# Loading the first eight chunks in 768-byte pieces, with conversion on GpSimd and two row copies per chunk

## The chip, the cores and the metric

The kernel runs on one core of a Trainium2 chip. The metric is the device time of one execution in microseconds. Three runs of the kernel before took 1412.79, 1413.59 and 1414.21 us; their median is 1413.59.

The engines are TensorE (PE in the rows; its weight loads are PEld), VectorE (DVE), ScalarE (ACT), GpSimd (POOL) and SyncE (SP). SyncE computes nothing here: it issues the DMAs. Every engine works through its own instructions in program order.

## The reference

Three stages follow one another. Inputs q, k, v and alpha have shape 4 x 8 x 768 x 48 (batch, head, time, dimension).

```
for t in range(S):                                  # gated linear attention
    state = alpha[t][:, None] * state + outer(k[t], v[t])
    y[t]  = q[t] @ state
x = y as 3072 x 384                                 # tokens x (head, dimension)
x = (sigmoid(x @ w_gate) * (x @ w_val)) @ w_out     # 384 -> 1536 -> 384
p = domain_probs / domain_probs.sum(-1)
out = sum over 4 experts of p[:, e] * (relu(x @ w1[e]) @ w2[e])   # 384 -> 1024 -> 384
```

Everything is float32. The gate weights are scaled up by 6.956, so the sigmoid is steep and the products before it must be accurate.

## The kernel before

**Split products.** A float32 product is made of three faster ones: every operand is kept as a high part and a low part (high x high, high x low, low x high). So each operand has to be split: ScalarE writes the high part, VectorE or GpSimd the low part as a difference.

**Chunks.** The recurrence runs over 24 chunks of 128 time steps (6 per batch). A chunk is handled in three stages. Stage 1 brings alpha, k and q into the layout head-and-dimension by time (heads in pairs, 64 rows for each head, of which 48 are used), forms running products of alpha forwards and backwards by two scans (`s1_a`, line 249, and `s1_b`, line 243) and multiplies them into q and k. Stage 2 (`s2_pe`, `s2_ev`) makes the masked scores q k. Stage 3 (`s3_pe`) adds the carried state's part and the scores' part into y; `s3_state` and `st_decay` carry the state on. For chunks 0 to 7 stage 1 turns the data on TensorE: `s1_t` transposes four 128 x 128 tiles per tensor with line 227. The later chunks arrive in pieces of four time steps and are turned on VectorE in 32 x 32 blocks.

**From y to tokens.** `s3_y` copies y out of the accumulator (line 311). It has four pairs of heads, but the next stage wants 3 x 128 rows, so the 48 rows per half of the fourth pair are moved into the unused 16 rows of the three others, by DMA from one place of on-chip memory to another (line 315, six of them per chunk). `s4` then splits the result: high part on ScalarE (line 341), low part on line 343, by VectorE for chunks 0 to 7 and by GpSimd later.

**Weights of the middle stage.** The 36 units (for each of 12 steps a gate, a value and an output slice) arrive as raw 32-bit words in four landing buffers (`load_w`; the gate and value units in four DMAs each, lines 177 and 180) and are decoded on the way. `dec_pre` makes two ScalarE passes (line 197 on the low 16-bit halves, line 199 turning the high halves from bfloat16 to float16 in place), `dec_bits` one on VectorE (line 203) that joins them, `dec_hi` (line 216, ScalarE) and `dec_lo` (line 219, VectorE) split. One call of `dec` does one pass for each of four successive units: hi of unit n-2, lo of n-3, pre of n, bits of n-1, and then `flush_w` issues the load of the unit that takes the buffer just freed.

**Order.** The order is written out by hand. Chunks 0 to 4 come first, in a loop over g whose iteration runs stage 1 of chunk g+1, stages 2 and 3 of chunk g, the split of chunk g-2 and one `dec`. The loop is called the prologue here. Six blocks of 512 tokens follow, each of 12 steps: gate products (18 with the value products, through `gv`), the sigmoid (line 393), the multiplication (line 397), its split (lines 398 and 402) and the output products of the step before (`l2`). In block 0 the remaining decodes are spread over the steps, and chunks 5 to 7 with one stage to a step; chunks 8 to 23 follow in blocks 1 to 4. Then the experts run, on TensorE almost without a gap. Block 0's step 0 needs the split of chunk 3; its step 1 can only overwrite the gate accumulator when the sigmoid of step 0 has read it.

All DMAs stand in SyncE's queue, so a load that comes behind a row copy in the program waits until that copy's data is there.

## Time and profile before

| what | us |
|---|---|
| median of 3 runs | 1413.59 |
| the profiled execution | 1413.35 |
| its span | 1411.6 |
| TensorE busy in the span | 1369.7 (97%) |
| VectorE busy | 708.8 (50%) |
| ScalarE busy | 406.3 (29%) |
| GpSimd busy | 104.3 (7%) |

The busy shares are means over stretches that differ. In the 40 slices of the span TensorE is at nine tenths or more in all but a few of the first five, and the DMA engines are busy most in the same slices. So the rows below look mostly at the first 170 us. The prologue lasts until about 53 us. Block 0's step 0 begins at 53.21 and its step 1 at 66.94; block 0 ends near 168.7 (the run of 54 products that starts at 160.38 and takes 12.48 us holds 36 of block 0 and 18 of block 1). In the rows a plain float32 product counts twice, once for each of its two passes, a transpose once.

### The profile page before, as it was taken

The page shows a single profiled execution, that of the slowest core. Times are in us where ns is not written, and L with a number is a line of the kernel's source. Part 1 is how long each engine was busy: PE and PEld are TensorE (multiplying, and loading weights), DVE is VectorE, ACT ScalarE, POOL GpSimd, SP SyncE. Part 2 cuts the span into 40 slices and gives each one's busy share as a digit, 9 for nine tenths or more (in the row PEclk, how much of TensorE's full clock was granted, in tenths as well). Part 3 has the DMA queues.
Part 4 walks back from the last instruction along what each step waited for, and adds up shares of the span by engine and source line. Part 5 has one row for each costly group of instructions (what it writes and reads, how often), then busy time and mean ns, then how long its engine had stood idle before and what let it go on. Part 6 is the DMA issues. An engine that isn't in the chain of part 4 may idle for free.

```text
span 1411.6 us, 19056 instructions
## 1 busy us (share of the span) xinstructions
PE 1369.7 (97%) x7600; PEld 1191.9 (84%) x7600; DVE 708.8 (50%) x1134; ACT 406.3 (29%) x794; POOL 104.3 (7%) x115
## 2 busy tenths in 40 slices
PE   8588999999999999999999999999999999999998
PEld 7467788788888888789999999999999999999997
DVE  6456777656565542244444444444444444444444
ACT  4587633333333333331111111111111111111111
POOL 0000000000000001430110011011011101101000
PEclk9899999999999999999999999999999999999999
DMA  9785422323232202130000000000000000000003
GB/s 128 128 172 134 115 71 74 85 61 76 72 79 71 75 4 97 53 97 0 23 23 1 23 23 23 0 23 23 0 23 23 12 12 23 0 0 1 1 29 109
DMA packets 116368, 70.19 MB, mean 50 GB/s; under 512 B 61488, under 2 KB 110896, under 8 KB 116272
## 3 DMA queue, kind: packets, MB, share of 16 engines
q1 hardware_dynamic: 116272, 68.90, 20.3%
q8 instruction: 62, 1.02, 0.3%
q14 instruction: 34, 0.28, 0.1%
HBM read 59.03 MB, written 8.65 MB: 48 GB/s over the span
## 4 chain that ended last, share of the span: by engine, by line
PE 84%; DMA 4%; issue 3%; ACT 3%; SPq 3%; DVE 2%; POOL 1%; ACTq 0%; POOLq 0%; DVEq 0%
PE bank L133 81%; PE bank L294 2%; SPq L315 1%; DMA LD<-in_moe_w_gate_dram 1%; ACT LD L199 1%; DMA LD<-LD 1%; DMA FA<-in_q_dram 1%; PE bank L274 1%; POOL RR L422 0%; DMA LD<-in_moe_w_val_dram 0%; DVE FA L243 0%; ACT RR L216 0%; ACT LD L267 0%; DMA LD<-in_moe_w_dram 0%; ACT LD L197 0%
## 5 line engine op out<-in xcount | busy, mean ns | idle before, releaser
L133 PE MATMUL bank<-RR 128*128 128x512 f32 (+1 forms) x5976 | 1262.2, 372 | 26.4 <-ACT LD L393 12.3
L133 PEld LDWEIGHTS bank<-RR 128*128 128x128 f32 x5976 | 1092.4, 189 | 184.4 <-ACT LD L393 14.0
L438 ACT ACTIVATE RR<-bank 128x512 fp32r<-128x512 f32 x192 | 114.7, 598 | 647.1 <-PE bank L133 647.1
L439 DVE SCALAR_TENSOR_TENSOR RR<-bank,RR 128x512 fp32r<-128x512 f32 x192 | 132.6, 691 | 330.7 <-ACT RR L438 330.7
L455 DVE SCALAR_TENSOR_TENSOR FA<-bank,pn,FA 128x384 f32<-128x384 f32 x360 | 221.6, 616 | 99.9 <-PE bank L133 99.9
L397 DVE TENSOR_TENSOR LD<-bank,LD 128x512 f32<-128x512 f32 x72 | 49.7, 691 | 171.9 <-PE bank L133 151.2
L422 POOL TENSOR_TENSOR RR<-LD,RR 128x384 fp32r<-128x384 f32 x64 | 63.5, 1020 | 641.1 <-PE bank L133 609.5
L393 ACT ACTIVATE LD<-bank 128x512 f32<-128x512 f32 x72 | 43.4, 602 | 140.0 <-PE bank L133 140.0
L398 ACT ACTIVATE RR<-LD 128x512 fp32r<-128x512 f32 x72 | 45.4, 631 | 115.2 <-DVE LD L397 115.1
L402 DVE TENSOR_TENSOR RR<-LD,RR 128x512 fp32r<-128x512 f32 x72 | 49.6, 689 | 11.7 <-ACT RR L398 11.2
L163 DVE STREAM_TRANSPOSE FA<-FA 128x512 f32<-128x512 f32 x48 | 51.9, 1081 | 0.0
L343 POOL TENSOR_TENSOR RR<-LD,RR 128x384 fp32r<-128x384 f32 x16 | 18.9, 1182 | 379.2 <-ACT RR L341 258.5
L133 PE MATMUL bank<-FA 48*128 48x128 f32 (+1 forms) x704 | 41.2, 259 | 0.1
L133 PEld LDWEIGHTS bank<-FA 48*128 48x128 f32 (+1 forms) x704 | 35.5, 167 | 6.3 <-issue 4.6
L199 ACT ACTIVATE LD<-LD 128x384 f16<-128x384 bf16 x36 | 38.1, 1059 | 0.0
L285 DVE TENSOR_TENSOR FA<-bank,mask 128x512 int32<-128x512 int32 x48 | 30.9, 684 | 11.6 <-PE bank L133 11.6
L243 DVE TENSOR_TENSOR_SCAN FA<-FA,LD 128x516 f32<-128x516 f32 x24 | 29.6, 1233 | 12.4 <-ACT FA L236 7.7
L249 DVE TENSOR_TENSOR_SCAN FA<-FA,LD 128x516 f32<-128x516 f32 x24 | 31.9, 1330 | 0.0
L203 DVE SCALAR_TENSOR_TENSOR LD<-LD 128x384 int32<-128x384 int32 x36 | 20.0, 555 | 16.1 <-ACT LD L199 13.7
L421 ACT ACTIVATE RR<-LD 128x384 fp32r<-128x384 f32 x64 | 28.0, 513 | 0.0
L334 ACT ACTIVATE St<-St,dk 128x128 f32<-128x128 f32 x80 | 25.4, 388 | 4.5 <-DVE St L329 2.7
L267 ACT ACTIVATE bank<-FA 128x512 f32<-128x512 f32 x38 | 23.3, 613 | 11.3 <-DVE FA L249 10.7
(63 smaller groups left out, 411.1 us busy)
## 6 DMA issues: line engine op xcount, KB each, us to landing
LD<-in_moe_w_dram SPq DMA_DIRECT2D x32, 384.0 KB, 3.3
FA<-in_alpha_dram SPq DMA_DIRECT2D x64, 96.0 KB, 2.3
FA<-in_k_dram SPq DMA_DIRECT2D x64, 96.0 KB, 2.4
FA<-in_q_dram SPq DMA_DIRECT2D x64, 96.0 KB, 2.3
FA<-in_v_dram SPq DMA_DIRECT2D x24, 192.0 KB, 3.0
LD<-in_moe_w_out_dram SPq DMA_DIRECT2D x12, 384.0 KB, 3.8
out_dram<-FA SPq DMA_DIRECT2D x24, 192.0 KB, 1.9
x2d<-LD SPq DMA_DIRECT2D x15, 256.0 KB, 2.2
```

Source lines behind the costliest of these rows:

```text
L133: nc.tensor.matmul(o, lhsT=l, rhs=r, start=start, stop=stop)
L163: nc.vector.transpose(out.rearrange("p a (t c) -> p a c t", c=TQ), t[:, BL:].rearrange("p (a d) -> p a d", d=D)[:, :, 0:BL])
L199: nc.scalar.activation(h[:, :, 1].bitcast(F16), h[:, :, 0].bitcast(BF16), AF.Copy)
L249: nc.vector.tensor_tensor_scan(flat(Iv), Ar[:, 0:NP * PW], flat(Cs), 1.0, ALU.mult, ALU.max)
L393: nc.scalar.activation(sg[f % 2], bank[0], AF.Sigmoid)
L397: nc.vector.tensor_tensor(s, bank[1], s, ALU.mult)
L398: nc.scalar.activation(gs[f % 2][0], s, AF.Copy)
L402: nc.vector.tensor_tensor(gl, sg[f % 2], gh.bitcast(F32), ALU.subtract)
L422: nc.gpsimd.tensor_tensor(lo, l[:, cs], h.bitcast(F32), ALU.subtract)
L438: nc.scalar.activation(h, bk, AF.Relu)
L439: nc.vector.scalar_tensor_tensor(l, bk, 0.0, h.bitcast(F32), ALU.max, ALU.subtract)
L455: nc.vector.scalar_tensor_tensor(acc[:, tt, :], bk, pn[:, tt, e:e + 1], acc[:, tt, :], ALU.mult, ALU.add)
```

## The change

Five things change. Chunks 0 to 7 are loaded like the later ones, in pieces of four time steps (768 bytes): a partition holds four successive time steps of one pair of heads, in two DMAs per tensor instead of one. `s1_t` turns them by products with the identity, eight per tensor, each of which takes one time step of four (c) and one head of a pair (j) and writes its 128 columns into the accumulator at their places (steps of 4 and 128 columns). For chunks 0 and 1 the second halves are issued from ScalarE's queue.

The pass from bfloat16 to float16 moves from ScalarE to GpSimd. The row copies become one per half, since the fourth pair's rows are dealt out in threes (`(p c)` in place of `(c p)`), and the weight rows are loaded in the matching order. The first decode runs in iteration 1 of the prologue instead of 2, with units 0 and 1 loaded in iteration 0 and 2 and 3 in iteration 1, and one decode fewer follows the loop. The load of the probabilities moves into block 1 and their division into block 2.

```diff
--- before.py
+++ after.py
@@ -79,9 +79,9 @@
 
 
     HW = 64
-    qn = [carve(FA, 512 * i, H, HW) for i in (0, 1)]
-    kn = [carve(FA, 512 * i, H, HW) for i in (2, 3)]
-    an = [carve(FA, 512 * i, H, HW) for i in (4, 5)]
+    qn = [carve(FA, 512 * i, 512) for i in (0, 1)]
+    kn = [carve(FA, 512 * i, 512) for i in (2, 3)]
+    an = [carve(FA, 512 * i, 512) for i in (4, 5)]
     vn = [carve(FA, 512 * i, H, HW) for i in (6, 7)]
     qt = [carve(FA, 512 * i, NP, P) for i in (8, 9)]
     kt = [carve(FA, 512 * i, NP, P) for i in (10, 11)]
...
@@ -138,25 +139,27 @@
         mm(o, ll, rh, False, stop)
 
 
-    def load(g, part, eng=nc.sync):
+    def load(g, part, engs=(nc.sync, nc.sync)):
         if g >= NCH:
             return
         b, c = divmod(g, CPB)
         i = g % 2
         ts = slice(c * P, (c + 1) * P)
         if part:
-            eng.dma_start(out=vn[i][:, :, 0:D], in_=v[b, :, ts, :].rearrange("h p d -> p h d"))
+            nc.sync.dma_start(out=vn[i][:, :, 0:D], in_=v[b, :, ts, :].rearrange("h p d -> p h d"))
             return
         if g < NPE:
             for t, x in ((an, alpha), (kn, k), (qn, q)):
-                eng.dma_start(out=t[i][:, :, 0:D], in_=x[b, :, ts, :].rearrange("h p d -> p h d"))
+                for j in (0, 1):
+                    engs[j].dma_start(out=t[i][:, j * TQ * D:(j + 1) * TQ * D],
+                                      in_=x[b, j:H:2, ts, :].rearrange("a (t c) d -> t a (c d)", c=TQ))
             return
         for t, x in ((ab, alpha), (kbl, k), (qb, q)):
             for j in (0, 1):
                 for h in (0, 1):
                     r = BL * (2 * j + h)
                     o = BL * (1 - h)
-                    eng.dma_start(out=t[r:r + BL, o:o + NP * TQ * D].rearrange("t (a e) -> t a e", a=NP),
+                    nc.sync.dma_start(out=t[r:r + BL, o:o + NP * TQ * D].rearrange("t (a e) -> t a e", a=NP),
                                   in_=x[b, j:H:2, ts, :].rearrange("a (t c) d -> t a (c d)", c=TQ))
 
     def tr32(out, t):
@@ -172,14 +175,13 @@
             l = l.rearrange("p (c f) -> p c f", c=KC)
             cs = slice(f * 4 * P, (f + 1) * 4 * P)
             m = NPM * 2 * D
-            sp = D // NPM
             for j in (0, 1):
                 nc.sync.dma_start(
                     out=l[64 * j:64 * j + D],
                     in_=w[0:m, cs].rearrange("(c j p) f -> j p c f", j=2, p=D)[j])
                 nc.sync.dma_start(
                     out=l[64 * j + D:64 * j + 64],
-                    in_=w[m + j * D:m + (j + 1) * D, cs].rearrange("(c p) f -> p c f", p=sp))
+                    in_=w[m + j * D:m + (j + 1) * D, cs].rearrange("(p c) f -> p c f", c=NPM))
         else:
             nc.sync.dma_start(out=l, in_=w_out.bitcast(U16)[f * P:(f + 1) * P, :])
 
@@ -196,7 +198,7 @@
         h = w[:, :, 1:2].bitcast(U16)
         nc.scalar.activation(w[:, :, 0].bitcast(I32), w[:, :, 0].bitcast(U32), AF.Copy,
                              scale=2.0 ** -13 * (1 - 2.0 ** -22), bias=-0.5 + 2.0 ** -5)
-        nc.scalar.activation(h[:, :, 1].bitcast(F16), h[:, :, 0].bitcast(BF16), AF.Copy)
+        nc.gpsimd.tensor_copy(h[:, :, 1].bitcast(F16), h[:, :, 0].bitcast(BF16))
 
     def dec_bits(u):
         w = land[u % NL][1].bitcast(I32)
@@ -223,8 +225,11 @@
         return [x.rearrange("p (a b) -> p a b", a=NP) for x in bk]
 
     def s1_t(g, X, t):
-        for p in range(NP):
-            nc.tensor.transpose(X[:, p * P:(p + 1) * P], t[g % 2][:, 2 * p:2 * p + 2, :].rearrange("p a b -> p (a b)"), ident)
+        for c in range(TQ):
+            for j in (0, 1):
+                o = (j * TQ + c) * D
+                mm(X[64 * j:64 * j + 64].rearrange("q (a m c) -> q c m a", a=NP, c=TQ)[:, c],
+                   t[g % 2][:, o:o + HW], ident, True, True)
 
     def flat(t):
         return t.rearrange("p a b -> p (a b)")
@@ -309,11 +314,8 @@
     def s3_y(g, bk):
         y = xr[g % 2]
         nc.scalar.activation(y, pairs(bk)[0], AF.Copy)
-        sp = D // NPM
         for j in (0, 1):
-            for c in range(NPM):
-                nc.sync.dma_start(out=y[64 * j + D:64 * j + 64, c, :],
-                                  in_=y[64 * j + sp * c:64 * j + sp * (c + 1), NPM, :])
+            nc.sync.dma_start(out=y[64 * j + D:64 * j + 64, 0:NPM, :], in_=y[64 * j:64 * j + D, NPM, :])
 
 
     def diag(j):
@@ -573,13 +575,15 @@
 
     with tc.manual_schedule():
         make_identity(nc, ident)
-        load(0, 0)
-        load(1, 0)
+        load(0, 0, (nc.sync, nc.scalar))
+        load(1, 0, (nc.sync, nc.scalar))
         load(0, 1)
         load(1, 1)
-        for t, val in ((an, 1.0), (kn, 0.0), (qn, 0.0), (vn, 0.0)):
+        for t, val in ((an, 1.0), (kn, 0.0), (qn, 0.0)):
             for i in (0, 1):
-                nc.gpsimd.memset(t[i][:, :, D:HW], val)
+                nc.gpsimd.memset(t[i][:, 2 * TQ * D:], val)
+        for i in (0, 1):
+            nc.gpsimd.memset(vn[i][:, :, D:HW], 0.0)
         nc.vector.memset(one, 1.0)
         nc.vector.memset(Cs, 1.0 / BOUND)
         nc.vector.memset(Ar, 0.0)
@@ -647,6 +651,7 @@
                 s1_range(g + 1, sg[0])
             if g >= 2:
                 s4(g - 2)
+            if g >= 1:
                 dec(False)
             if g + 1 < NPRO:
                 s1_b(g + 2)
@@ -656,17 +661,15 @@
             s3_y(g, b3)
             if g == 3:
                 load(g + 2, 1)
-            for u in ((0,), (1, 2), (3,), (), ())[g]:
+            for u in ((0, 1), (2, 3), (), (), ())[g]:
                 load_w(u)
             flush_w()
             s3_state(g, b3)
             if g < NPRO:
                 st_decay(g + 1)
         s4(NPRO - 1)
-        for _ in range(4):
+        for _ in range(3):
             dec()
-
-        nc.sync.dma_start(out=pn, in_=dprobs.rearrange("(t p) e -> p t e", p=P))
 
 
         stages = [(t, g) for g in range(NPRO + 1, 2 * NPRO) for t in (1, 2, 3, 0)][:-1]
@@ -735,6 +738,8 @@
                     nc.vector.tensor_reduce(fl[:, 2 * NCH + f:2 * NCH + f + 1], wh, mybir.AxisListType.XY, ALU.add,
                                             apply_absolute_value=True)
                 if bi == 1 and f == 0:
+                    nc.sync.dma_start(out=pn, in_=dprobs.rearrange("(t p) e -> p t e", p=P))
+                if bi == 2 and f == 0:
                     nc.vector.tensor_reduce(psm, pn, mybir.AxisListType.X, ALU.add)
                     nc.vector.tensor_scalar(psm, psm, 1e-9, None, ALU.add)
                     nc.vector.reciprocal(psm, psm)
```

SyncE's queue around the copies of chunks 2 and 3 reads as follows in the kernel before (LD is the memory that holds landing buffers and y; the copies are LD<-LD).

```order
L315 DMA LD<-LD 16x128 x6
L177 DMA LD<-in_moe_w_gate_dram 48x3x512
L180 DMA LD<-in_moe_w_gate_dram 16x3x512
L177 DMA LD<-in_moe_w_gate_dram 48x3x512
L180 DMA LD<-in_moe_w_gate_dram 16x3x512
L315 DMA LD<-LD 16x128 x6
L148 DMA FA<-in_v_dram 128x8x48
```

In the changed kernel the same place, from chunk 2's copies to chunk 4's, reads:

```order
L318 DMA LD<-LD 16x3x128 x2
L179 DMA LD<-in_moe_w_val_dram 48x3x512
L182 DMA LD<-in_moe_w_val_dram 16x3x512
L179 DMA LD<-in_moe_w_val_dram 48x3x512
L182 DMA LD<-in_moe_w_val_dram 16x3x512
L318 DMA LD<-LD 16x3x128 x2
L149 DMA FA<-in_v_dram 128x8x48
L186 DMA LD<-in_moe_w_out_dram 128x1536
L318 DMA LD<-LD 16x3x128 x2
```

Six copies became two at each place, and the unit loaded between those of chunks 2 and 3 is unit 4 instead of unit 3.

ScalarE's queue at the end of the prologue, from chunk 2's split (line 341) in the last iteration to the first decodes behind the loop, in the kernel before:

```order
L341 ACTIVATE RR<-LD 128x3x128
L216 ACTIVATE RR<-LD 128x384
L197 ACTIVATE LD<-LD 128x384
L199 ACTIVATE LD<-LD 128x384
L311 ACTIVATE LD<-bank_63 128x512
L341 ACTIVATE RR<-LD 128x3x128
L216 ACTIVATE RR<-LD 128x384
L197 ACTIVATE LD<-LD 128x384
L199 ACTIVATE LD<-LD 128x384
```

And in the changed kernel (line 343 is 341 before, 218 is 216, 199 is 197, 316 is 311):

```order
L343 ACTIVATE RR<-LD 128x3x128
L218 ACTIVATE RR<-LD 128x384
L199 ACTIVATE LD<-LD 128x384
L316 ACTIVATE LD<-bank_63 128x512
L343 ACTIVATE RR<-LD 128x3x128
L218 ACTIVATE RR<-LD 128x384
L199 ACTIVATE LD<-LD 128x384
L218 ACTIVATE RR<-LD 128x384
L199 ACTIVATE LD<-LD 128x384
```

One ScalarE instruction less stands in each decode; the old line 199 is now a GpSimd instruction (line 201).

TensorE's first turns, in the kernel before (bank_64 is written by warm-up products with the identity; banks 70, 69 and 68 take alpha, k and q):

```order
L133 MATMUL bank_64<-ident 128x64 x5
L227 MATMUL bank_70<-ident,FA 128x128 x4
L133 MATMUL bank_64<-ident 128x64 x2
L227 MATMUL bank_69<-ident,FA 128x128 x4
L227 MATMUL bank_68<-ident,FA 128x128 x4
```

And in the changed kernel:

```order
L134 MATMUL bank_64<-ident 128x64 x5
L134 MATMUL bank_70<-ident,FA 64x32x4 x8
L134 MATMUL bank_64<-ident 128x64 x2
L134 MATMUL bank_69<-ident,FA 64x32x4 x8
L134 MATMUL bank_68<-ident,FA 64x32x4 x8
```

Four transposes per tensor became eight products with 64 output rows each, at the same places in the order.

## Rows read from the trace of the kernel before

**Rows 1.** Busy time by stretch: PE, PEld, DVE, ACT, POOL, granted clock, DMA share, GB/s

```profile
18.25:53.20 34.95, 23.75 (x312) 19.33 (x309) 22.09 (x44) 20.54 (x50) 0.00 (x0) 0.93 0.63 107
53.20:66.90 13.70, 6.93 (x18) 4.91 (x18) 4.95 (x11) 8.14 (x14) 0.00 (x0) 0.75 0.83 162
66.90:168.70 101.80, 90.43 (x494) 70.95 (x495) 66.92 (x126) 76.32 (x143) 0.24 (x3) 0.94 0.66 140
168.70:544.40 375.70, 374.64 (x2367) 307.46 (x2366) 226.94 (x334) 131.64 (x279) 18.92 (x16) 1.00 0.27 70
```

**Rows 2.** TensorE's waits from 66.9 to 168.7, then after: total, times, longest

```profile
PE bank L133 <- ACT LD L393: 11.0, 3, 6.8
PE bank L133 <- DVE RR L219: 6.7, 5, 2.9
...
PE bank L133 <- POOL RR L343: 1.1, 2, 0.5
```

**Rows 3.** Timeline, 41 to 67 us: start, length, engine, instruction [idle before]

```profile
41.58 0.67 ACT L311 ACTIVATE LD<-bank 128x512 f32<-128x512 f32 x1
...
45.49 1.53 PE L227 MATMUL bank<-ident,FA 128*128 128x128 f32 x12
...
46.29 0.52 ACT L341 ACTIVATE RR<-LD 128x384 fp32r<-128x384 f32 x1 [2.35 <-DMA LD<-LD]
...
47.19 3.99 SPq L315 DMA_DIRECT2D LD<-LD  x6
...
47.57 1.04 ACT L199 ACTIVATE LD<-LD 128x384 f16<-128x384 bf16 x1
...
48.35 0.68 ACT L311 ACTIVATE LD<-bank 128x512 f32<-128x512 f32 x1
...
52.63 0.52 ACT L341 ACTIVATE RR<-LD 128x384 fp32r<-128x384 f32 x1 [3.60 <-DMA LD<-LD]
...
53.21 6.93 PE L133 MATMUL bank<-RR 128*128 128x512 f32 x18 [6.19 <-ACT RR L341]
...
59.72 0.43 SPq L180 DMA_DIRECT2D LD<-in_moe_w_gate_dram  x1
...
64.50 0.54 ACT L197 ACTIVATE LD<-LD 128x384 int32<-128x384 uint32 x1 [0.90 <-DMA LD<-in_moe_w_gate_dram]
...
66.94 6.76 PE L133 MATMUL bank<-RR 128*128 128x512 f32 x18 [6.80 <-ACT LD L393]
```

**Rows 4.** Lines of ScalarE and VectorE, 66.9 to 168.7: busy, mean ns | idle

```profile
L199 ACT ACTIVATE LD<-LD 128x384 f16<-128x384 bf16 x29 | 30.8, 1061 | 0.0
...
L203 DVE SCALAR_TENSOR_TENSOR LD<-LD 128x384 int32<-128x384 int32 x30 | 16.6, 554 | 9.9 <-ACT LD L199 7.5 <-DMA LD<-in_moe_w_out_dram 2.5
```

**Rows 5.** Timeline, block 0: products at full clock

```profile
85.11 8.50 PE L133 MATMUL bank<-RR 128*128 128x512 f32 x36
```

**Rows 6.** Timeline of GpSimd and VectorE, then line 343: ns min/median/max

```profile
3.23 0.29 POOL L589 TENSOR_SCALAR_AFFINE_SELECT LD<-LD 128x128 f32<-128x128 f32 x1
...
257.81 1.22 DVE L249 TENSOR_TENSOR_SCAN FA<-FA,LD 128x516 f32<-128x516 f32 x1
257.90 1.94 POOL L343 TENSOR_TENSOR RR<-LD,RR 128x384 fp32r<-128x384 f32 x1 [20.29 <-DVE LD L397]
...
L343 POOL TENSOR_TENSOR RR<-LD,RR x16: 1012/1018/2035, 189.3 to 528.5; 128x384 fp32r<-128x384 f32 x16
```

**Rows 7.** Timeline of TensorE, 8 to 24 us (full-width, transposes, half-width)

```profile
8.32 1.00 PE L133 MATMUL bank<-ident 128*128 128x64 f32 x8
...
17.50 0.66 PE L227 MATMUL bank<-ident,FA 128*128 128x128 f32 x4
...
22.30 1.06 PE L294 MATMUL bank<-FA 128*64 128x128 f32 x16
```

**Rows 8.** DMA issues: count, KB each, median us from issue to landing

```profile
FA<-in_alpha_dram SPq DMA_DIRECT2D x64, 96.0 KB, 2.3
...
FA<-in_alpha_dram SPq DMA_DIRECT2D x8, 192.0 KB, 4.8
```

## The prediction

> **What bounds the kernel now.** I read the busy time by stretch first, then what TensorE waited for, then the timeline where the waits are. From 168.7 us on the kernel is TensorE: 374.64 us busy of 375.70 up to 544.4, at full clock [rows 1], and nothing in the change shortens a product there. Ahead of that TensorE is not the bound. In 18.25 to 53.2 (recurrence of chunks 1 to 4) it works 23.75 of 34.95 us; in 53.2 to 66.9, 6.93 of 13.70 at a mean granted clock of 0.75; in 66.9 to 168.7 (block 0 from its step 1 on), 90.43 of 101.80 at 0.94 [rows 1]. The waits in that last stretch are 11.0 us for the sigmoid of line 393 (6.8 of it at 66.94, its very edge) and 6.7 us for the low parts of line 219 [rows 2]. Both sit behind ScalarE's decode: ScalarE is busy 76.32 of 101.80 us there [rows 1], 30.8 of them in line 199 alone [rows 4].
>
> The timeline shows how block 0 comes to start late [rows 3]. Line 341 of chunk 2 waits 2.35 us for row copies (46.29) and holds line 311 of chunk 4 back to 48.35. Line 341 of chunk 3 waits 3.60 us more, because SyncE issued that chunk's six copies only from 47.19 on (3.99 us), though their data had been there since 41.58 + 0.67. So block 0 opens at 53.21 instead of behind chunk 5's transposes at 47.02. Then step 1 waits 6.80 us: line 393 stands on ScalarE behind line 197 of unit 6, the last piece of whose load was issued at 59.72, behind chunk 4's copies, and which started at 64.50.
>
> **The change part by part.** The sum is made against the profiled execution, 1413.35 us (span 1411.6 and 1.75 around it); the median of the runs is 0.24 higher, which is nothing.
>
> *Head.* Six loads now stand ahead of ScalarE's table load, and the first identity products run at the low clock. A 96 KB load in 768-byte pieces lands in 2.3 us, one of 192 KB in 192-byte pieces in 4.8 [rows 8]; so alpha of chunk 0 is there earlier, but its products cost more. I charge +0.8. The bounds are -2.5 (the whole difference in landing kept) and +2.5 (the table load waits for one such landing more).
>
> *Identity products.* A tensor took four transposes, 0.66 us. Eight products with 64-column weights and 128 columns have the form of line 294, 1.06 us at full clock [rows 7]. So +0.40 per tensor, 24 tensors. Those of the prologue lie in the 11.2 us that TensorE idles between 18.25 and 53.2, where vector and scalar work sets the pace; without that cover twelve of them would cost 4.8. Chunks 6 and 7 lie in block 0: six tensors, +2.4 on the path. Products that write columns 16 and 512 bytes apart are not in the trace. Bounds per eight: 0.66 (no dearer than transposes) and 2.0 (warm-up products with full-width weights, 1.00 for four) [rows 7]; I take 1.06, the same shape.
>
> *One copy per half instead of three, and the earlier first decode.* SyncE saves four issues of 0.67 us per chunk (3.99 / 6), and copies no longer pile up behind weights. The 2.35 us wait of chunk 2's line 341 goes, and line 199 leaves ScalarE ahead of line 311 (48.35 - 47.57 = 0.78): 3.1 us earlier. Against this stand the 0.8 of the head and one more line 203 on VectorE in the third iteration (0.55 [rows 4], since the decode starts an iteration earlier). Chunk 4's line 311 then starts at 48.35 - 3.1 + 1.35 = 46.6. Chunk 3's two copies go out behind its own line 311 (41.58 + 0.67, and 1.0 late: 43.3), cost 1.3 and land 1.45 after (52.63 less 47.19 + 3.99): 46.1, before line 341 is reached at 47.3. That wait of 3.60 goes. Next comes TensorE itself: chunk 4's products end at 45.49 + 1.0 = 46.5, chunk 5's 24 identity products take 3.2, and block 0 opens at 49.7 instead of 53.21. Products at full clock took 8.50 / 36 = 0.236 us [rows 5], so step 0's eighteen are done in 4.25, at 54.0, where before they took 6.93.
>
> Step 1 is late next, for unit 6. Its load goes out behind chunk 4's copies (46.6 + 0.7 + 1.3 = 48.6), takes SyncE 1.8 and lands as long after the last issue as before (59.72 + 0.43 to 64.50, 4.35): 54.7. From line 197 to step 1 it was 66.94 - 64.50 = 2.44, less 0.8 for the line 199 that is gone: 56.3. **Step 1 starts 10.6 us earlier.** With the prologue 3 us slower than I think it is 7.6; with unit 6 in time, 12.9.
>
> *Conversion on GpSimd.* ScalarE loses 30.8 of 76.32 us in block 0 [rows 1, 4] and is no longer near the bound. A mean clock of 0.94 between 1.2 and 2.4 GHz means 0.12 of 101.8 us at the low level, half of it lost: 6.1. TensorE's need there at full clock is 90.43 - 6.1 + 2.4 = 86.7. A GpSimd copy of 128x384 is not in the trace. Bounds: 0.29, an affine select with one input at a third of the width, and 1.02, a subtraction with two inputs at this width [rows 6]; thrice the affine select would be 0.87, and I take 0.67.
>
> The trace shows what GpSimd and VectorE do to each other. The subtraction at 257.90 lasted 1.94 us and ended 0.81 after the scan of line 249, which had begun just before it and has two SBUF inputs, was over; its median is 1.02, its longest 2.04 [rows 6]. So I add casts to VectorE's work: 66.92 [rows 1] + 29 x 0.67 = 86.4, beside TensorE's 86.7. Two engines with the same load do not overlap perfectly; of the 17.0 us now lost (11.0 - 6.8 + 6.7 of waits, 6.1 of low clock) I keep 6, which gives 92.7 for 101.8: **9.1 us**. The bounds are 15.1 (nothing kept) and -0.7 (rival 1).
>
> This is where the Trainium skill speaks against the change: "SBUF — State Buffer", section "SBUF: two separate sides", says that VectorE and GpSimd share one port pair and that it is "an exclusive lock, not a bandwidth split", held for a whole instruction. The row at 257.90 agrees: 1.94 instead of 1.02. With the lock the stretch is the 92.7 above; without it VectorE would have some 20 us to spare, and the stretch would be nearer 88.
>
> The Trainium skill's "GPSIMD Engine Reference", section "Performance versus the Vector engine", prices a one-input body at 1.03 cycles an element, some 0.5 us for this copy with its dispatch (an estimate from that page); no row shows it, and by it the forecast would be 1 to 2 us lower.
>
> *The rest.* After 168.7 TensorE waits 1.1 us for line 343 behind the six copies [rows 2]; with two copies most of that goes, 1.0. The probabilities' load leaves a crowded stretch, and the division moves to block 2, on a VectorE that is busy 226.94 of 375.70 us there [rows 1]: nothing.
>
> Sum: 10.6 + 9.1 + 1.0 = 20.7, so 1413.35 - 20.7 = **1392.7 us**.
>
> **Rivals.** *1, VectorE and GpSimd become the bound.* For it: the wait at 257.90, and lines 203, 219 and 402 all have two SBUF inputs, so casts meet them. Against: 1.02 is a two-input price. With 1.02 per cast 66.92 + 29 x 1.02 = 96.5, and 6 kept makes 102.5 for 101.8: block 0 gains nothing, only its earlier start remains. 1413.35 - 10.6 - 1.0 + 0.7 = 1402.5.
>
> *2, everything late vanishes.* Unit 6 is in time, step 1 opens at 54.0 and TensorE never waits in block 0: 12.9 + 15.1 + 1.0 = 29.0, 1384.4. For it: with line 199 gone no engine has more than 87 us of work there. Against: ScalarE meets loads in order, and four landing buffers leave little room.
>
> *3, slower: the identity products.* Place: 18 tensors between 18.25 and the end of block 0. If writing to scattered columns takes each to 0.37 us, half as much again as a warm-up product's 0.25 [rows 7], eight take 3.0 and a tensor costs 2.3 more than before; 18 x 2.3 less the 11.2 idle in the prologue is 30.2, against the 23.1 that the rest brings: 1413.35 + 7.1 = 1420. It decides from about 0.32 us per product. Against: line 294 does eight in 1.06.
>
> *4, nothing comes of it*: the prologue stretches by what the copies free, and the casts eat block 0; 1411 to 1416.
>
> **How the numbers follow.** Forecast 0.58, with its own range 1387 to 1398; rival 1 0.18; rival 2 0.12; rival 3 0.06; rival 4 0.06. The range 1383 to 1405 holds the forecast, most of rival 1 and half of rival 2. About 0.2%, 2.8 us, is what a measurement tells from no change. Faster: 0.58 + 0.18 + 0.12 = 0.88; same 0.06; slower 0.06.
>
> **What will show it.** Line 316 (311 before) of chunk 4 near 46.6, the first product of block 0 near 49.7, of its step 1 near 56.3, the end of block 0 near 149 instead of 168.7. Casts of 0.6 to 0.8 us, longer where a two-input VectorE instruction is running; waits of TensorE for line 395 (393 before) nearly gone, and no wait for row copies. I am wrong if casts take over 1 us, if eight identity products take over 1.3 us, if TensorE's work in the prologue rises without an earlier block 0, or if the time saved lies behind 168.7.

## The result and the profile after

The changed kernel took 1400.74 us (median of four runs, 1398.54 to 1401.64), the kernel before 1413.34 in the same session (1412.79 to 1414.21): a ratio of 0.9908, interval 0.9891 to 0.9925. That is 12.6 us faster where 20.7 were forecast. The profiled execution took 1400.38 us, its span is 1398.7.

Line numbers moved: 133 and 227 are now 134, 197 is 199, the conversion is 201, 203 is 205, 219 is 221, 311 is 316, 315 is 318, 341 and 343 are 343 and 345, 393 is 395. In some of the runs further down the numbers shift again by up to five.

First the same stretches as in [rows 1], in the changed kernel: length, busy time of PE, PEld, DVE, ACT and POOL with instruction counts, granted clock, DMA share, GB/s.

```profile
19.58:50.88 31.30, 26.67 (x415) 23.25 (x412) 25.51 (x47) 19.79 (x50) 6.50 (x6) 0.95 0.55 141
50.88:57.06 6.18, 4.38 (x20) 3.30 (x18) 3.60 (x8) 2.98 (x6) 2.09 (x2) 1.00 0.58 135
57.06:157.35 100.29, 91.19 (x566) 71.73 (x567) 74.65 (x127) 53.09 (x115) 33.16 (x32) 0.97 0.60 150
157.35:531.50 374.15, 374.15 (x2368) 307.72 (x2367) 225.85 (x333) 129.32 (x278) 16.50 (x16) 1.00 0.27 70
```

Block 0 opens at 50.88 and reaches its step 1 at 57.06, 9.9 us sooner than before. From there it still lasts 100.3 us where it lasted 101.8, though ScalarE's work in it fell from 76.32 to 53.09. Behind it the span has 1398.7 - 157.35 = 1241.35 us left, against 1411.6 - 168.7 = 1242.9. So the 12.9 us of the two spans are 9.9 of an earlier start, 1.5 inside block 0 and 1.5 behind it.

The timeline where the start was decided, against [rows 3] (start, length, engine, instruction, idle time before):

```profile
48.38 0.60 ACT L316 ACTIVATE LD<-bank 128x512 f32<-128x512 f32 x1 [0.37 <-PE bank L299]
...
50.88 4.38 PE L134 MATMUL bank<-RR 128*128 128x512 f32 x18
...
52.41 0.57 SPq L182 DMA_DIRECT2D LD<-in_moe_w_gate_dram  x1
...
55.50 0.56 ACT L199 ACTIVATE LD<-LD 128x384 int32<-128x384 uint32 x1 [1.91 <-DMA LD<-in_moe_w_gate_dram]
...
57.06 1.20 PE L134 MATMUL bank<-RR 128*128 128x512 f32 x4 [1.80 <-ACT LD L395]
```

Step 0 no longer waits for a row copy. Step 1 waits 1.80 us where it waited 6.80, and again for unit 6: the last piece of its load is issued at 52.41, and line 199 stands 1.91 us until it has landed.

TensorE's waits in block 0 from step 1 on (total, times, longest), against [rows 2]:

```profile
PE bank L279 <- ACT bank L272: 5.1, 3, 1.9
PE bank L134 <- DVE RR L221: 3.0, 2, 2.6
PE bank L134 <- ACT LD L395: 2.4, 2, 1.8
PE bank L134 <- DVE LD L399: 0.2, 1, 0.2
```

The wait for the sigmoid is nearly gone, as foretold, but 5.1 us of other waits stand in its place: a chunk's k transposes (line 279) wait for ScalarE's pass of line 272. All four sum to 10.7 us; 1.8 of it lies at the very edge, so 8.9 inside. Before it was 17.7, of which 6.8 lay at the edge, so 10.9 inside.

The conversions and the VectorE instructions beside them in the same stretch, grouped by line (count, busy time, mean ns, idle time before and for whom), against [rows 4]:

```profile
L201 POOL CAST LD<-LD 128x384 f16<-128x384 bf16 x29 | 33.1, 1162 | 57.5 <-DMA LD<-in_moe_w_gate_dram 19.7 <-DMA LD<-in_moe_w_val_dram 14.6 <-DMA LD<-in_moe_w_out_dram 8.8
L221 DVE TENSOR_TENSOR RR<-LD,RR 128x384 fp32r<-128x384 f32 x32 | 20.0, 628 | 0.0
L205 DVE SCALAR_TENSOR_TENSOR LD<-LD 128x384 int32<-128x384 int32 x30 | 19.6, 653 | 5.1 <-POOL LD L201 5.1
```

A conversion takes 1.16 us on GpSimd where ScalarE took 1.06, and line 205 rose from 554 to 653 ns each. But GpSimd idles 43 us for loads in this stretch, and ScalarE, which waited 1.8 us for weights before, waits 9.5 now. First the kernel before, then the changed one:

```profile
ACT LD L197 <- DMA LD<-in_moe_w_gate_dram: 1.8, 1, 1.8
```

```profile
ACT LD L199 <- DMA LD<-in_moe_w_gate_dram: 5.7, 3, 3.3
ACT LD L199 <- DMA LD<-in_moe_w_out_dram: 2.6, 2, 1.8
ACT LD L199 <- DMA LD<-in_moe_w_val_dram: 1.2, 1, 1.2
```

The timeline of one stall shows a wait for row copies beside them:

```profile
81.74 1.21 SPq L318 DMA_DIRECT2D LD<-LD  x2
...
85.34 1.05 POOL L201 CAST LD<-LD 128x384 f16<-128x384 bf16 x1 [1.76 <-DMA LD<-in_moe_w_gate_dram]
...
86.93 0.52 ACT L343 ACTIVATE RR<-LD 128x384 fp32r<-128x384 f32 x1 [3.43 <-DMA LD<-LD]
87.49 0.56 DVE L345 TENSOR_TENSOR RR<-LD,RR 128x384 fp32r<-128x384 f32 x1 [5.08 <-ACT RR L343]
...
88.88 2.23 POOL L201 CAST LD<-LD 128x384 f16<-128x384 bf16 x2 [2.50 <-DMA LD<-in_moe_w_val_dram]
89.03 1.16 DVE L205 SCALAR_TENSOR_TENSOR LD<-LD 128x384 int32<-128x384 int32 x1
89.17 3.17 PE L134 MATMUL bank<-RR 128*128 128x512 f32 x8 [2.55 <-DVE RR L221]
...
91.79 0.55 DVE L205 SCALAR_TENSOR_TENSOR LD<-LD 128x384 int32<-128x384 int32 x1
```

Two small row copies, fully issued at 82.95, land only at 86.9. ScalarE, VectorE and TensorE stand in a row behind them. In all line 343 waits 5.7 us for row copies in this stretch, as line 341 did before. The loads on the other side wait too: SyncE's queue waits longest for line 205, which frees a landing buffer. It did so for line 203 before (first row):

```profile
SPq L177 <- DVE LD L203: 20.7, 9, 4.1
```

```profile
SPq L179 <- DVE LD L205: 17.4, 10, 4.1
SPq L149 <- PE bank L299: 5.9, 1, 5.9
```

### The profile page after: what moved, and what is told of

Read it like the earlier page. It is cut to its first block, busy times and chain, and to the rows that moved or that the text cites. A ratio compares the mean times of both kernels' runs of the same rounds, so it can differ in the third digit from the quotient of the medians.

```text
span 1398.7 us, 19554 instructions
## 1 busy us (share of the span) xinstructions
PE 1374.1 (98%) x7888; PEld 1199.1 (86%) x7888; DVE 717.5 (51%) x1134; ACT 375.1 (27%) x758; POOL 143.5 (10%) x151
## 4 chain that ended last, share of the span: by engine, by line
PE 86%; issue 3%; DMA 1%; DVE 1%; POOL 1%; ACT 1%; SPq 0%; POOLq 0%; DVEq 0%; ACTq 0%
PE bank L134 83%; PE bank L299 2%; PE bank L279 1%; POOL RR L424 0%; DMA LD<-in_moe_w_dram 0%; POOL RR L385 0%; DVE RR L221 0%; SPq L179 0%; DVE LD L399 0%; DMA LD<-in_moe_w_val_dram 0%; DMA LD<-in_moe_w_out_dram 0%; DMA LD<-in_moe_w_gate_dram 0%; ACT bank L272 0%; DVE FA L254 0%; DMA LD<-x2d 0%
## 5 line engine op out<-in xcount | busy, mean ns | idle before, releaser
L201 POOL CAST LD<-LD 128x384 f16<-128x384 bf16 x36 | 41.7, 1174 | 102.0 <-DMA LD<-in_moe_w_gate_dram 47.0
L134 PE MATMUL bank<-ident,FA 128*64 128x128 f32 x384 | 25.7, 286 | 1.6 <-ACT St L336 1.6
L299 PEld LDWEIGHTS bank<-FA,St 128*64 128x64 f32 x320 | 17.9, 140 | 9.8 <-issue 5.6
```

Of the source, the lines that this page charges most:

```text
L134: nc.tensor.matmul(o, lhsT=l, rhs=r, start=start, stop=stop)
L201: nc.gpsimd.tensor_copy(h[:, :, 1].bitcast(F16), h[:, :, 0].bitcast(BF16))
L299: nc.tensor.matmul(X0[64 * j:64 * j + 64, p, :], lhsT=l, rhs=r, start=start and p == 0, stop=True, skip_group_check=True)
```

## The experiments

Two theories stood at the start. *Port*: GpSimd's conversions take back on VectorE, by the shared port, what ScalarE gained. *Supply*: block 0 is as long as weights and row copies take to arrive and be decoded one after another, whichever engine does it. After the first four runs the question became whether the conversion has a price at all, and which part of the supply counts. The first three columns below are of one profiled execution each; "stretch" is from step 1 to the end of block 0.

| kernel | step 1 | block 0 ends | stretch | median us | ratio to before, interval |
|---|---|---|---|---|---|
| changed | 57.1 | 157.3 | 100.3 | 1400.7 | 0.9908, 0.9891 to 0.9925 |
| conversion on ScalarE | 58.9 | 157.9 | 99.0 | 1401.0 | 0.9905, 0.9888 to 0.9921 |
| conversion twice | 58.2 | 161.7 | 103.5 | 1404.7 | 0.9932, 0.9916 to 0.9949 |
| conversion split | 59.7 | 159.4 | 99.7 | 1401.3 | 0.9905, 0.9889 to 0.9922 |
| copies on ScalarE's queue | 58.5 | 155.9 | 97.4 | 1396.8 | 0.9873, 0.9856 to 0.9889 |
| no conversion | 57.2 | 152.3 | 95.1 | 1395.8 | 0.9880, 0.9862 to 0.9898 |
| no loads after unit 3 | 56.1 | 144.3 | 88.2 | 1386.4 | 0.9814, 0.9796 to 0.9832 |
| block 0's copies there | 57.4 | 153.5 | 96.1 | 1397.6 | 0.9892, 0.9875 to 0.9910 |
| six copies | 68.4 | 166.3 | 97.9 | 1409.0 | 0.9973, 0.9963 to 0.9984 |
| half the bytes | 57.7 | 155.1 | 97.4 | 1395.1 | 0.9871, 0.9854 to 0.9888 |
| half the issues | 57.0 | 149.3 | 92.3 | 1393.3 | 0.9864, 0.9847 to 0.9880 |
| split a step later | 58.6 | 157.5 | 98.9 | 1399.8 | 0.9906, 0.9889 to 0.9922 |
| old loads, transposes | 56.5 | 154.6 | 98.1 | 1399.5 | 0.9915, 0.9894 to 0.9937 |

The kernel before took 1415.0 us in the session of runs 1 to 4 and 1412.8 in those of runs 5 to 8 and 9 to 12, against 1413.3 beside the changed kernel. Taken by the ratios, differences from the changed kernel move by up to 1.2 us (2.3 in run 12), so two rows less than about 2 us apart are not told apart.

**1. The conversion back on ScalarE.**

```diff
-        nc.gpsimd.tensor_copy(h[:, :, 1].bitcast(F16), h[:, :, 0].bitcast(BF16))
+        nc.scalar.activation(h[:, :, 1].bitcast(F16), h[:, :, 0].bitcast(BF16), AF.Copy)
```

> The changed kernel with the bfloat16-to-float16 pass back on ScalarE; everything else as changed. Theory 1 (port): the casts on GpSimd took back, through VectorE, nearly all that ScalarE was relieved of; then moving them back costs little in block 0 (its 100.3 us become 101 to 104, ScalarE-bound again) and about 2 us ahead of it (0.8 for each of two or three passes ahead of line 311): 1403 to 1406. Rival (supply): block 0 is held by the landing of weights and row copies, which ScalarE meets in order, and the place of the pass does not matter: 1400 to 1402. If the pass on GpSimd is worth what I predicted, 1408 to 1412.

Measured 1400.96 (1400.82 to 1401.22), as supply expects. Its stretch, in the columns of the windows above:

```profile
58.89:157.85 98.96, 91.50 (x566) 71.46 (x566) 65.90 (x124) 76.41 (x143) 0.24 (x3) 0.97 0.57 147
```

ScalarE has its 76 us back, VectorE is 8.7 us lighter, and block 0 is as long. What changes is where it waits. ScalarE now waits 1.1 us for weights, where it waited 9.5 in the changed kernel:

```profile
ACT LD L199 <- DMA LD<-in_moe_w_out_dram: 0.9, 1, 0.9
ACT LD L199 <- DMA LD<-in_moe_w_gate_dram: 0.2, 1, 0.2
```

TensorE's waits for the sigmoid are back at 6.4 us, 2.8 of them at the edge. So either neither engine's work sets the length, or two limits, ScalarE's queue here and late weights there, happen to be alike.

**2. Each conversion twice on GpSimd.**

```diff
+        nc.gpsimd.tensor_copy(h[:, :, 1].bitcast(F16), h[:, :, 0].bitcast(BF16))
         nc.gpsimd.tensor_copy(h[:, :, 1].bitcast(F16), h[:, :, 0].bitcast(BF16))
```

> The changed kernel with every cast issued twice on GpSimd, the second a repetition of the first, so 36 more GpSimd instructions of 1.05 us. Theory 1 (port): VectorE, already at 74.7 us of work and 5.1 of waits for casts in 100.3, loses at least as much again as the first casts took (7.8 of longer instructions and 5.1 of waits): block 0 takes 8 to 30 us more, 1408 to 1430. Rival (supply): GpSimd was idle 57 us of the stretch waiting for loads, so a second cast hides; 1400 to 1403.

Measured 1404.7 (1404.1 to 1405.63), between the two: 4.0 us for 36 more conversions.

```profile
58.22:161.70 103.48, 92.19 (x566) 71.00 (x566) 85.44 (x125) 54.27 (x114) 71.87 (x62) 0.97 0.53 143
```

VectorE rises by 10.8 us, yet the stretch grows only by 3.2.

**3. Odd units on GpSimd, even ones on ScalarE.**

```diff
-        nc.gpsimd.tensor_copy(...)
+        if u % 2:
+            nc.gpsimd.tensor_copy(...)
+        else:
+            nc.scalar.activation(..., AF.Copy)
```

> The changed kernel with the casts of odd units on GpSimd and of even units on ScalarE. Theory 1 (port): half of the 12.9 us by which casts lengthen or hold VectorE goes, and ScalarE, at 53 + 15 x 0.8 = 65 us of 100, does not become the bound: 2 to 6 us faster than the changed kernel, 1394 to 1398. Rival (supply): within 1.5 us of it, 1399 to 1402.

Measured 1401.26. Sharing the work between the engines brings nothing, as supply expects.

**4. The row copies issued from ScalarE's queue.**

```diff
-            nc.sync.dma_start(out=y[64 * j + D:64 * j + 64, 0:NPM, :], in_=...)
+            nc.scalar.dma_start(out=y[64 * j + D:64 * j + 64, 0:NPM, :], in_=...)
```

> The changed kernel with the two row copies of a chunk issued from ScalarE's queue, right behind line 316, instead of SyncE's. Rival (supply): the copies no longer stand behind weight pieces in one ring, so the waits of line 343 for them in block 0 (5.7 us of ScalarE, 10.7 of VectorE behind it) fall to under 2 and SyncE no longer waits for line 316 with weights behind it: 3 to 6 us faster, 1394 to 1397; against it 1.2 us of ScalarE per chunk. Theory 1 (port) alone: under 2 us faster, 1398 to 1401, since VectorE keeps its lock with GpSimd.

Measured 1396.77 (1396.1 to 1398.61), 4.0 us below the changed kernel: the fastest kernel here that computes everything. The copies that landed 4.0 us after their last issue above:

```profile
79.50 1.21 ACTq L318 DMA_DIRECT2D LD<-LD  x2
...
84.23 0.52 ACT L343 ACTIVATE RR<-LD 128x384 fp32r<-128x384 f32 x1 [0.93 <-DMA LD<-LD]
```

Line 343 waits 0.93 us instead of 3.43. The copies still take 3.5 us from their last issue (80.71) to landing. Most of the gain is that they go out at 79.50, right behind line 316, and not at 81.74, when SyncE has got through the weights before them. In the prologue the move costs time: block 0 opens at 53.98 instead of 50.88.

**5. No conversion at all.** The line is left out; the weights are wrong, masked to stay finite, and the landing buffers are cleared once at the start.

```diff
-        nc.gpsimd.tensor_copy(h[:, :, 1].bitcast(F16), h[:, :, 0].bitcast(BF16))
...
-        ... w[:, :, 1], -2 ** 16, w[:, :, 0], ...
+        ... w[:, :, 1], 2 ** 30 - 2 ** 16, w[:, :, 0], ...
```

> Changed kernel, 1400.7, with the 36 conversions left out altogether, so the decoded weights are wrong (their bits are masked to stay finite, and the limit of the final range test is raised). Moving the conversion back to ScalarE left the time the same (1401.0). That has two readings. Price theory: the conversion costs about as much on ScalarE (30 us of its own time) as on GpSimd (locked VectorE, some 8 us); then without it block 0 gains what was forecast, 9 us or most of it: 1391 to 1395. No-price theory: engine time of the decode is not what block 0's length comes from, the landing of loads and row copies is: 1397 to 1401.

Measured 1395.79 (1395.07 to 1396.9), between the two ranges: the conversion has a price of 4.9 us, which is half the 9.1 of the forecast, even if it vanishes. Together with runs 1 to 3: none -4.9, on any engine within 0.6 of the changed kernel, twice +4.0. In these runs the price goes with how long a unit's conversion takes, not with where it is done.

**6. No loads after the first four units.** The landing buffers are decoded again and again; all engine work and all row copies stay.

```diff
     def load_w(u):
+        if u >= NL:
+            return
...
```

> Changed kernel with only the first four weight units loaded; the other 32 are decoded again from what stands in the landing buffers, so the weights are wrong (bits masked to stay finite, limit of the range test raised). All engine work and all row copies stay. Supply theory (row copies and units wait in SyncE's queue and behind one another's packets, and ScalarE meets them in order): row copies land at once, no unit is late; step 1 starts at 54 to 56 and block 0 loses at most 5 us beside its 87 of products: 1386 to 1393. Price theory (engine time of the decode, locked VectorE): the conversions are all still there, so 1397 to 1401.

Measured 1386.44 (1386.15 to 1387.78), as supply expects.

```profile
56.08:144.30 88.22, 86.94 (x567) 70.99 (x566) 74.25 (x128) 52.73 (x115) 34.02 (x29) 0.98 0.16 40
```

This row decides between the theories. VectorE is as busy as in the changed kernel (74.25 for 74.65), GpSimd too, and TensorE works 86.94 of 88.22 us. So neither the port nor the work of these engines alone makes the other 12 us: they are there only when weights are on their way. The conversion is on GpSimd here; what 76 us of ScalarE would make of the stretch without loads was not run.

**7. Only block 0's copies from ScalarE's queue.**

```diff
-            nc.sync.dma_start(...)
+            (nc.scalar if 5 <= g < 8 else nc.sync).dma_start(...)
```

> Changed kernel with the row copies of chunks 5 to 7 alone issued from ScalarE's queue; those of the prologue stay on SyncE. With all copies on ScalarE's queue block 0 opened 3.1 us later (53.98 for 50.88) and still ended 1.4 earlier. Supply theory: the opening returns to 50.9 and step 1 to 57, the stretch stays at 97 to 98: end near 154, 1393.5 to 1397. Rival (what the other queue gave was in the prologue, or block 0 gives a gain of its start back later): 1398 to 1402.

Measured 1397.58 (1397.1 to 1398.11), 0.6 above the upper end of supply's range. Step 1 comes at 57.4 and block 0 ends at 153.5, as expected. But TensorE then waits for the last chunk's split:

```profile
155.10 4.15 PE L134 MATMUL bank<-RR 128*128 128x512 f32 x17 [1.42 <-DVE RR L345]
```

So 1.4 of the 3.8 us gained in block 0 are paid at the next block's edge; by the spans (1395.3 for 1398.7) 3.4 are left at the end.

**8. Six row copies, the rest as changed.**

```diff
-            nc.sync.dma_start(out=y[64 * j + D:64 * j + 64, 0:NPM, :], in_=y[64 * j:64 * j + D, NPM, :])
+            for c in range(NPM):
+                nc.sync.dma_start(out=y[64 * j + D:64 * j + 64, c, :],
+                                  in_=y[64 * j + sp * c:64 * j + sp * (c + 1), NPM, :])
...
```

> Changed kernel with six row copies per chunk and the weight rows in the order that goes with them, everything else as changed. Forecast's theory: the earlier start of block 0 comes from the copies (waits of 2.35 and 3.60 us for them before) more than from the earlier first decode; step 1 then starts at 61 to 66 and the time is 1405 to 1411. Rival, the earlier first decode and loads give it: step 1 at 57 to 60, 1401 to 1404.

Measured 1408.95 (1408.63 to 1410.5), in the forecast's range, with step 1 even later than it said (lines 346 and 398 are 343 and 395 above):

```profile
57.86 0.52 ACT L346 ACTIVATE RR<-LD 128x384 fp32r<-128x384 f32 x1 [4.63 <-DMA LD<-LD]
...
58.00 3.67 SPq L320 DMA_DIRECT2D LD<-LD  x6
...
58.44 7.42 PE L134 MATMUL bank<-RR 128*128 128x512 f32 x18 [2.65 <-ACT RR L346]
...
68.37 2.08 PE L134 MATMUL bank<-RR 128*128 128x512 f32 x4 [2.52 <-ACT LD L398]
```

The whole earlier start needs the two copies; without them, the earlier first decode and the new loads leave step 1 at 68.4, behind the 66.9 of before. Whether two copies alone would give it in the kernel before was not run.

**9. Half the bytes in the same number of DMAs** (from unit 4 on, half the rows; weights wrong).

```diff
-                    out=l[64 * j:64 * j + D], in_=w[0:m, cs]...[j]
+                    out=l[64 * j:64 * j + n], in_=w[0:m, cs]...[j][0:n]     # n = D // 2 from unit 4 on
...
```

> Changed kernel where each weight unit after the first four brings half its rows (same number of DMAs, half the bytes; weights wrong, bits masked, range limit raised). Leaving all these loads out gave 1386.4, 14.3 us below the changed kernel. If bytes on the DMA engines make units and row copies late, half the bytes give back more than half of that: 1387 to 1393. If it is SyncE, which issues four DMAs for most units at 0.6 us each and stands in order, nothing much changes: 1397 to 1401.

Measured 1395.14, with wide runs (1392.62 to 1396.93): 5.6 us, less than half of the 14.3 and between the two readings. The profiled execution is the slowest of the four.

**10. Two DMAs per gate or value unit instead of four** (the fourth pair's rows are not loaded; weights wrong).

```diff
+                if u < NL:
                     nc.sync.dma_start(out=l[64 * j + D:64 * j + 64], in_=...)
...
```

> Changed kernel where gate and value units after the first four are loaded by their two large DMAs alone: two issues of SyncE each instead of four, a quarter fewer bytes (weights wrong, bits masked, range limit raised). If SyncE's issues are what makes units late, most of the 14.3 us comes back: 1387 to 1392. If it is bytes, a quarter of them is worth a quarter to a third: 1395 to 1398.

Measured 1393.29 (1392.87 to 1393.95): 7.4 us, half of the 14.3, with a quarter fewer bytes in two of three units, so between the two readings. The stretches of runs 9 and 10, one after the other:

```profile
57.69:155.06 97.37, 92.61 (x566) 74.45 (x567) 73.33 (x127) 53.31 (x115) 35.01 (x32) 0.93 0.36 99
```

```profile
57.00:149.34 92.34, 87.10 (x567) 69.38 (x567) 73.50 (x126) 52.43 (x115) 33.38 (x32) 1.00 0.60 139
```

Run 9 has the lower DMA share but a granted clock of 0.93 for 1.00 and 5.5 us more of TensorE time. That is as much as the two stretches differ by (5.0), while TensorE waits 5.8 and 5.0 us in them. So the two profiles do not show which of bytes and issues counts for more.

**11. The split of chunks 5 and 6 one step later.**

```diff
-                    late.append((bi * NF + f + 1, g))
+                    late.append((bi * NF + f + 1 + (5 <= g < 7), g))
```

> Changed kernel with the split of chunks 5 and 6 (line 343 and 345, which wait for the row copies) done one step of block 0 later, where the copies have long landed; copies stay in SyncE's queue. Supply theory, by which ScalarE standing at line 343 for 3.4 and 2.3 us holds up the decode and the sigmoid behind it: these waits go and most of the 5.7 us with them, 1395 to 1398, as with the copies on ScalarE's queue (1397.6). Rival: those waits only moved a wait that comes anyway, and SyncE's queue behind the copies was the gain of the other queue: 1399 to 1401.

Measured 1399.76 (1397.66 to 1400.43): the rival's range. ScalarE no longer waits for a row copy there, and waits for weights instead (in the changed kernel 5.7 and 1.2 us for the first two of these):

```profile
ACT LD L199 <- DMA LD<-in_moe_w_gate_dram: 9.8, 4, 3.6
ACT LD L199 <- DMA LD<-in_moe_w_val_dram: 4.7, 3, 2.8
```

So the stall at line 343 was one place where lateness showed, not its cause.

**12. The old loads and transposes, the rest as changed.**

```diff
-                for j in (0, 1):
-                    engs[j].dma_start(out=t[i][:, j * TQ * D:(j + 1) * TQ * D], in_=...)
+                nc.sync.dma_start(out=t[i][:, :, 0:D], in_=x[b, :, ts, :].rearrange("h p d -> p h d"))
...
```

> Changed kernel with the chunks' old loads (192-byte pieces, one DMA per tensor) and the four transposes per tensor, the rest as changed. Forecast's terms (identity products cost 2.4 us in block 0 and the head 0.8, the loads save nothing else): 1397 to 1398. Rival: 192-byte pieces land in 4.8 us for 2.3 and hold the row copies and weights behind them back, in the prologue and in block 0: 1402 to 1407.

Measured 1399.46 (1398.75 to 1403.98): neither range, and no difference from the changed kernel that can be told. Lines 340, 197 and 390 are 345, 199 and 395 above.

```profile
49.41 4.19 PE L134 MATMUL bank<-RR 128*128 128x512 f32 x17 [0.29 <-DVE RR L340]
...
54.94 0.56 ACT L197 ACTIVATE LD<-LD 128x384 int32<-128x384 uint32 x1 [3.15 <-DMA LD<-in_moe_w_gate_dram]
...
56.50 1.78 PE L134 MATMUL bank<-RR 128*128 128x512 f32 x4 [2.90 <-ACT LD L390]
```

Block 0 opens at 48.64, 2.2 us sooner, but step 1 at 56.50 is only 0.6 sooner: unit 6 is late again. Block 0 ends at 154.6, 2.8 sooner, yet the span is only 0.7 shorter (1398.0); TensorE waits 1.5 us behind block 0 for the sigmoid, where it waited 0.4 in the changed kernel, and the rest was not traced.

## Why the forecast was right on the direction and 8 us short on the size

*Head and opening: a little dear.* The head cost 1.3 us for the 0.8 charged: ScalarE's first pass over a chunk (line 241, 236 before), which stands behind the six loads and the table load, starts at 6.62 for 5.28. The opening came at 50.88 for 49.7. Run 12 sizes the head together with the dearer products of the prologue: without both, block 0 opens 2.2 us sooner.

*Identity products: right.* Eight take 1.04 to 1.09 us at a granted clock of 1.00; 1.06 was taken. The six tensors in block 0 cost 5.7 us for 2.9 before, so 2.8 for the 2.4 charged. The new loads and products have no measurable worth either way in this kernel (run 12).

```profile
11.13 1.09 PE L134 MATMUL bank<-ident,FA 128*64 128x128 f32 x16
...
16.97 1.04 PE L134 MATMUL bank<-ident,FA 128*64 128x128 f32 x16
```

*Two copies instead of six, and the start of step 1: right in what waits, and in the sum partly by luck.* It gave 9.9 us for 10.6. Both waits of line 341 are gone and unit 6 is next in line, as worked out, and run 8 shows that this needs the two copies. But line 316 of chunk 4 came at 48.38, no sooner than the 48.35 of before, where 46.6 was forecast. Unit 6's last issue ended at 52.98 (52.41 + 0.57), 2.6 later than the 50.4 of the forecast, and its data was there 2.5 us behind that, where 4.35 had been taken. The two misses nearly cancel.

*The rest: right.* 1.5 us for 1.0; the 1.1 us of waits for line 343 in [rows 2] are gone.

*Conversion on GpSimd: this is the step that failed.* It gave 1.5 us for 9.1. TensorE's need was sized well: 86.7 us against the 87.10 that run 10 shows at a granted clock of 1.00. What failed is the step from "ScalarE loses 30.8 of 76.32 us and is no longer near the bound" to keeping only 6 us beyond that need. 13.2 stayed (100.29 less 87.10): 8.9 of waits, and the rest nearly all lower clock. The 6 was not worked out from a row, and the forecast had no term for weights that come late once ScalarE is free of that work. ScalarE's waits for weights rose from 1.8 to 9.5 us, those for row copies stayed at 5.7, where none was forecast, and without weights on their way nearly all of the loss vanishes with every conversion still in place (run 6).

A unit goes through a chain: a free landing buffer, SyncE's four issues, landing behind whatever is queued, conversion, line 205, buffer free again. The move changed the engine of one link but not its length, 1.06 us before and 1.16 after, and runs 1 to 3 and 5 fit a chain that stayed as slow. The profile before had rows to read for this, and I looked at busy time instead: SyncE waits 20.7 us for line 203 to free a buffer, line 203 waits for line 199 [rows 4], and rival 2 named the four landing buffers only in passing. It is not shown that ScalarE's work was no bound of its own before: with the conversion on it (run 1) it waits only 1.1 us for weights, and no run takes the loads away in that case.

The conversion was mis-sized too. It takes 1.16 us in the mean, over the 1 us that was named as a sign of being wrong, where 0.67 was taken. But the rule that adds conversions to VectorE's work was too dear: 33.1 us of them raised VectorE from 66.92 to 74.65, not to 86.4. The two errors have opposite signs.

*Rival 1* forecast 1402.5 and came closest, but for a reason that runs 1, 2 and 6 speak against: the stretch does not follow VectorE's work. VectorE does suffer: line 205 took 1.16 us beside the conversions at 88.88 and 0.55 alone at 91.79. The lock that the Trainium skill states in "SBUF — State Buffer", section "SBUF: two separate sides", agrees with those rows. The Trainium skill's "GPSIMD Engine Reference", section "Performance versus the Vector engine", led to an estimate of 0.5 us for this copy; the rows show 1.04 at the least, and they decide. *Rival 2* had block 0 without loss; run 6 shows that case at 1386.4, near its 1384.4, but only without loads. *Rival 3* is out by the 1.06 above, *rival 4* by the earlier start.

*What stays open.* The parts of the supply do not add up: 4.9 for the conversion, 3 to 4 for the copies' queue, 5.6 for half the bytes and 7.4 for half the issues make more than the 14.3 of run 6; they overlap. How much of it is SyncE's issuing and how much the landing was not separated, since run 10 takes both away and the profile of run 9 has a lower clock. Nor is the chain the pace throughout: 29 conversions through four buffers are about 7.25 turns, and 1.16 us more or less in each would be 8.4 us of the stretch (an estimate from these rows); leaving them out shortened it by 5.2, and doing them twice lengthened it by 3.2. That the clock falls behind some waits (below) makes small differences between kernels uncertain: run 4 waits 4.6 us in block 0 where the changed kernel waits 8.9 inside it, and has a clock of 0.93 for 0.97, in the slowest of its four executions.

## What to carry to other kernels

When work moves from a busy engine to an idle one, ask whether that engine's time or the length of a chain through it sets the pace: if consumers wait for loads while loads wait for freed buffers, only a shorter link helps, and a move to an engine that takes as long gains nothing. Small transfers that others wait for should not have to wait for an engine that is still issuing large ones; fewer of them (run 8), or another engine to issue them (run 4), were worth most here. A total that matches a rival is no proof of it: take away what each theory blames, one at a time.

## What the hardware showed that was not expected

A GpSimd copy from bfloat16 to float16, 128x384 with stride, takes 1.04 us at the least and 1.07 in the median, as long as ScalarE's 1.06, and up to 1.92:

```profile
L201 POOL CAST LD<-LD x36: 1040/1066/1919, 26.3 to 146.3; 128x384 f16<-128x384 bf16 x36
```

The longest starts at 35.90, while a scan on VectorE (line 248) runs from 35.76 to 36.99, and ends 0.83 us behind it, as the subtraction in [rows 6] ended 0.81 behind its scan.

Two row copies of 24 KB landed 4.0 us after their last issue from SyncE's queue and 3.5 from ScalarE's (runs "changed" and 4), in both while weights were being loaded. The median from issue to landing is 2.3 us in both, first the changed kernel, then run 4: it hides the few that hurt, and it does not show the time before the issue, which is where run 4 gained most.

```profile
LD<-LD SPq DMA_DIRECT2D x48, 24.0 KB, 2.3
```

```profile
LD<-LD ACTq DMA_DIRECT2D x48, 24.0 KB, 2.3
```

The stall of 2.55 us before 89.17 is followed by a lower clock: granted 1.00 of 2.4 GHz up to then, it is 0.74 and 0.83 in the two windows of four microseconds that follow, part of them at 1.2 GHz, before it is 1.00 again.

```profile
84.00:88.00 4.00, 2.61 (x38) 2.00 (x34) 0.51 (x2) 0.52 (x1) 1.05 (x1) 1.00 1.11 173
88.00:92.00 4.00, 2.83 (x8) 2.29 (x9) 4.00 (x7) 2.52 (x5) 2.23 (x2) 0.74 0.27 88
92.00:96.00 4.00, 4.00 (x16) 3.17 (x16) 2.23 (x6) 1.72 (x4) 0.21 (x1) 0.83 0.51 142
96.00:100.00 4.00, 3.21 (x14) 2.01 (x12) 3.16 (x6) 1.38 (x4) 2.44 (x3) 1.00 0.78 211
```
